# One chunk's residual on VectorE, an earlier load and sum of phi, and two pieces of TensorE work half a half slot later, in a one-core attention and mixer kernel

## The chip, the core and the metric

The kernel runs on one core of one Trainium2 chip. The core has a matrix engine (TensorE, PE in the profile, with PEld for its weight loads), three engines for elementwise work (VectorE or DVE, ScalarE or ACT, GpSimd or POOL), and SyncE (SP), which here only issues transfers. Each engine runs its own instructions in the order in which the program gives them, and waits at an instruction until what that needs is there. Transfers are issued by SP and by ACT and carried out by 16 DMA engines. The metric is the device time in microseconds of one execution, as the median of several.

## What is computed

The reference takes q, k, v and phi of 8 batches, 8 heads, 576 positions, and four weight matrices. Everything is in 32-bit floats.

```python
a = np.exp(phi - np.max(phi, axis=2, keepdims=True))        # over the 576 positions
a = a / (np.sum(a, axis=2, keepdims=True) + 1e-09)
k_m = np.einsum('bhsm,bhsd->bhmd', a, k)                    # 32 memory keys, 64 wide
v_m = np.einsum('bhsm,bhsd->bhmd', a, v)
scores = scale * np.matmul(q, k_m.transpose(0, 1, 3, 2))
attn = softmax(scores)                                      # over the 32 memories
x = np.matmul(attn, v_m)                                    # to (batch, 576, 512)
h = np.maximum(x.transpose(0, 2, 1) @ w_tok1, 0.0) @ w_tok2
u = x + h.transpose(0, 2, 1)
out = u + np.maximum(u @ w_ch1, 0.0) @ w_ch2                # 512 -> 1536 -> 512
```

## The kernel before

There are two streams of work. The first, by **quads**, is the attention and the token mixer: a quad is four heads of one batch, named (b, Q) with Q 0 or 1. The second, by **chunks**, is the channel mixer: the 8 x 576 positions are cut into nine chunks of 512, and each goes through the two big products with w_ch1 and w_ch2. The channel mixer is nearly all of TensorE's work, and the quads' small products are put in between.

Numbers are split into a high and a low part (`h`, `l`), each a float that the matrix engine's fast mode takes; a product is three matmuls, high by high, high by low, low by high. ScalarE makes the high part (a copy with rounding), VectorE or GpSimd the low part (a subtraction).

**The order.** Up to the end of chunk 0 a planner in the program orders the steps. After that the order is written out by hand. Time is counted in half slots h, 24 to a chunk. For chunks 1 and 2 a slot g covers h = 2g and 2g + 1: the first product of a hidden block (`ch1`, 12 matmuls into `cp`), then the second product of the block before it (`ch2`, 12 matmuls into `acc`). From h = 72 (chunk 3 on) `quarters` runs instead: it makes two hidden blocks at a time from seven smaller products (a recursive scheme on quarters of the matrices; tiles `qa`, `qb`, copied to `whole` by ScalarE), with the weights combined beforehand and loaded as `unit` tiles, issued by ScalarE, three ahead of their use.

Everything else is an event: `at(h, fn, *x, k=...)` enters a function under half slot h and a class k, and `run(h, ...)` calls what stands there. In a slot of chunk 1 or 2 `run` is called in this order: (2g - 1, 1), (2g - 0.5; -1, 0, 1), then the hidden block's high and low parts, (2g, 0), then `ch2`, then (2g, 1), (2g + 0.5; -1, 0, 1), (2g + 1; -1, 0). So an event at an even h with k = 0 is ahead of `ch2`, and with k = 1 behind it. Events of one h and k are called as they were entered, quad by quad.

**A quad's steps.** Each quad has a start m for its keys and values and a start r for its scores. The list `starts` (L1779 to L1782) gives, as (b, Q, m, r): (2, 0, 24, 24), (2, 1, 34, 34), (3, 0, 38, 44), (3, 1, 49, 54), (4, 0, 59, 63.5), (4, 1, 69, 74), (5, 0, 79, 86), (5, 1, 91, 98), and so on every 12 half slots to (7, 1, 139, 146). The steps, in the order in which data flows:

- `load_phi` (L405, a load of 320 KB on SP; two buffers, used in turn), `phi_max` (VectorE reduces over a partition's positions, then GpSimd does an all-reduce over partitions, `pr` and `prr`), `phi_sub` and `phi_only_exp`, `phi_sum` (the same with a sum, `pr` and `psr`).
- `step_kv` (L463): 40 small matmuls of phi by k and v into `kvp`. From quad (5, 0) on they stand inside `step_s` of the quad before (`follow`), at its r + 2. Then `spread_k`, at once for batch 2, later for the others (`scales`, `turn_keys`, `spread_v`, at m + 0.5 to m + 1.5). `turn_keys` stores the keys with four transfers on SP, `get_keys` at m + 3.5 loads them twice (`kb`). For batch 2 `step_T` at m + 1 turns them on TensorE (`Tp`). `load_kv` and `load_q` are on SP too.
- `step_s` at r + 2: scores into two banks `sp`; `turn_both` has VectorE turn them to `S` (L573), then `S_max`, `S_sub` (L583), `S_exp` on ScalarE, `S_sum`, `S_mul` (r + 2.5 to r + 4.5).
- `rows_out` at r + 4.5: four stores of S to DRAM on SP, and `rows_in` at r + 6, which loads them back as `raw` (L670, L673); `nat_full` and `nat_tail` (r + 8, r + 8.5) split `raw` into `nat`, on ScalarE and VectorE.
- `turn_pairs` at r + 5: `aT`; `a_pair` (L636) at r + 6 and r + 6.5: ScalarE copies the high part of one half of `aT` (L638), and GpSimd subtracts for the low part (L639). `v_pair` at r + 7 and r + 7.5: four ScalarE copies into `vv`, a tile that takes the room of `aT`, so they wait until `a_pair` has read it.
- `step_A` at r + 9.5 (needs `nat`), `step_R` at r + 10.5, and `step_u` in four parts from r + 12, 8 matmuls each into a bank `u`. ScalarE and VectorE take the result into the chunks' inputs `uh`, `ul` (or `u` and `rest`).

The small products share two PSUM banks (tag "at"), given out in turn: `kvp`, `Tp`, the two `sp`, `Ap`, `Rp` and each part of `u` take one, and wait until VectorE and ScalarE have read what was in it two takers ago.

**A chunk's end.** `residual` (L192) adds the two parts of the chunk's input again, four additions of 128 x 512, into a tile `o`; `add` (L200) adds the accumulated products when the chunk is done, and `store` writes it out. Chunks from 3 on keep their input whole and have no residual. For chunk 1 the residual stands at h = 44, for chunk 2 at h = 64 (`h - 8`), both on GpSimd.

The functions that the change touches, with the line numbers of the profile:

Of the kernel before, what the change touches and what calls it, by code (L numbers as in the profile page):

```python
# [28 lines left out]
def kernel(  # L29
# [25 lines left out]
    nc = tc.nc  # L55
# [10 lines left out]
    NF = 2 * w_ch2.shape[0]  # L66
# [3 lines left out]
    NKK = DM // P  # L70
# [5 lines left out]
    WIN, AHEAD = 3, 3  # L76
# [38 lines left out]
    def f32(t):  # L115
        return t.bitcast(F32)
# [16 lines left out]
    def wide(dtype, name):  # L133

        return sb.tile([P, NKK, CW], dtype, tag="wide", name=name, bufs=5)


    class Chunk:
# [50 lines left out]
                        stop=f == end - 1 and x == 2,  # L189
                    )  # L190

        def residual(s, channels=range(NKK)):  # L192
            for a in channels:
                if a == 0:
                    s.o = wide(F32, "o" + s.n)
                nc.gpsimd.tensor_tensor(
                    out=s.o[:, a], in0=f32(s.uh[:, a]), in1=f32(s.ul[:, a]), op=ALU.add
                )

# [127 lines left out]
    chunks = {}  # L327
# [1318 lines left out]
    a, c = quads[0, 0], quads[0, 1]  # L1646
# [80 lines left out]
    for Q, h0 in ((0, 3), (1, 11)):  # L1727
        qd = quads[1, Q]
# [46 lines left out]
    def at(h, fn, *x, k=0):  # L1775
        events.setdefault((max(h, 0), k), []).append((fn, x))
# [3 lines left out]
    while starts[-1][:2] != (B - 1, 1):  # L1780
        b, Q, m, r = starts[-1]
        starts.append((b + Q, 1 - Q, r + 5, r + NF))  # L1782
    for b, Q, m, r in starts:
        qd = second if b == 2 and not Q else Quad(b, Q)
        fine = b > 2
        if qd is not second:
            at(max(m - 11, 2 * NF), qd.load_phi)
            if fine:
                w = 1.5 * ((b, Q) == (5, 0))
                at(m - (6 if (b, Q) == (3, 0) else 8.5 - w), qd.phi_max, k=1)  # L1790
                w -= 1.5 * (JOINT < (b, Q))
                at(m - 4.5 + w, qd.phi_sub)
                at(m - 4 + w, qd.phi_only_exp)
                w += 1.5 * (JOINT < (b, Q))
                at(m - 3.5 + w, qd.phi_sum)
            else:
                at(m - 7, qd.phi_max, k=1)
                at(m - 3, qd.phi_exp, k=1)
                at(m - 2, qd.phi_sum, k=1)
            at(loaded + (5 if (b, Q) > (3, 1) else 1), qd.load_kv, k=1)  # L1800
            at(r - (3 if fine else 4), qd.load_q, k=1)
        joint = JOINT < (b, Q)
        if joint:
            former.follow, loaded = qd, m - 3
        else:
            at(m, qd.step_kv)
            loaded = m
        qd.follow, former = None, qd
        at(r + 2, qd.step_s)
        if fine:  # L1810
            for x, fn in (
                (m + 0.5, qd.scales), (m + 1, qd.turn_keys), (m + 1.5, qd.spread_v),
                (m + 3.5, qd.get_keys), (m + 5, qd.v_high), (m + 6, qd.v_low),
                (r + 2.5, qd.S_max), (r + 3, qd.sub_exp), (r + 4, qd.S_sum), (r + 4.5, qd.S_mul),
                (r + 4.5, qd.rows_out), (r + 5, qd.turn_pairs), (r + 8, qd.nat_full),
                (r + 8.5, qd.nat_tail), (r + 9.5, qd.step_A), (r + 10.5, qd.step_R),
            ):
                at(x, fn)
            at(r + 6, qd.rows_in, "qT", 1)
            for x in range(2):  # L1820
                at(r + 6 + x / 2, qd.a_pair, x)
                at(r + 7 + x / 2, qd.v_pair, x)
            for x in range(4):
                at(r + 12 + x // 2 * 1.5 + x % 2 / 2, qd.step_u, x // 2, x % 2)
            continue
        at(m + 4, qd.values)
        at(m + 1, qd.step_T)
        at(r + 3, qd.sm2)
        at(r + (3 if qd is second else 4), qd.a_pair, 1)
        at(r + 6, qd.nat, k=1)  # L1830
        at(r + 7, qd.v_pairs)
        at(r + 8, qd.step_A)
        at(r + 9, qd.step_R)
        for x in range(4):
            at(r + 10 + x // 2 * (1 if qd is second else 2), qd.step_u, x // 2, x % 2)
    for c in range(2, CHUNKS):
        h = 2 * NF * (c - 1)
# [18 lines left out]
    for c in range(CHUNKS - 1):  # L1856
        h = 2 * NF * (c + 1)
        if 0 < c < WIN:
            at(h - (8 if c == WIN - 1 else 4), lambda c=c: chunks[c].residual(), k=1)
        for x in range(NKK) if c < WIN - 1 else ():  # L1860
            at(h + 1, lambda c=c, x=x: chunks[c].add(x), k=-1)
        at(h + (3 if c < WIN - 1 else 4), lambda c=c: chunks[c].store(), k=1)
# [16 lines left out]
    for g in range(NF, NF * WIN):  # L1879
        c, f = g // NF, g % NF  # L1880
# [184 lines left out]
```

## Time and profile before

| what | us |
|---|---|
| median of 3 runs | 767.47 (766.58 to 768.25) |
| the profiled execution, whole | 765.93 |
| its span, first to last instruction | 764.1 |
| PE busy in it | 750.2 |
| DVE, ACT, POOL busy in it | 465.5, 338.2, 109.4 |
| mean granted PE clock | 0.997 |

The views that follow in the prediction are read like this. A row of the **timeline** gives the start in us from the span's start, the duration, the engine, the line, the operation, the tiles as out<-in with shapes, how many instructions were merged, and in brackets the engine's idle time before it with what ended that. A row of the **chain of waits** gives start, duration and what was running, for the work that ended last, followed back from the end. A row of the **waits** names who waited for whom, the total, the number of times and the longest. A row of the **groups** gives busy time and mean ns of one, and the idle time before them. A row of the **transfers** gives the queue that issued them, their number, the size of one and the median us from issue to landing. A q behind an engine's name is its sequencer, which issues transfers and waits. A releaser is inferred from the semaphores; where it had long been done, something else kept the engine. In time, h = 34 is near 165 us, h = 66 near 283 us, h = 72 near 303 us, and the phi maxima of the last four quads are at 387, 428, 469 and 511 us.

### The profile page before, as it was taken

What the parts mean: (1) busy time and instruction counts of PE and PEld (TensorE: products, weight loads), DVE (VectorE), ACT (ScalarE), POOL (GpSimd) and SP (SyncE); (2) the same over time, 40 slices, a digit from 0 to 9 for tenths busy, and PEclk for the clock granted to TensorE, in tenths of its full rate; (3) what the DMA queues carried; (4) which work ended last, traced back from release to release, by engine and by line L of the source; (5) the groups of instructions that cost most, each with busy time, mean ns of one, the idle gap of its engine ahead of it and who ended that gap; (6) DMA issues with size and microseconds to landing.
All of it is one profiled execution on the core that took longest, in us unless ns stands there. A gap on an engine that the chain in (4) does not pass through costs nothing.

```text
span 764.1 us, 13364 instructions
## 1 busy us (share of the span) xinstructions
PE 750.2 (98%) x5159; PEld 651.8 (85%) x5159; DVE 465.5 (61%) x876; ACT 338.2 (44%) x771; POOL 109.4 (14%) x94
## 2 busy tenths in 40 slices
PE   9999999999999999899999999999999999999998
PEld 8777788787877878789888889888989999998997
DVE  4989874787567655665676558554855255335234
ACT  5897553242414333454453536353635343333331
POOL 2144343011212123020101001010101000000000
PEclk9999999999999999999999999999999999999999
DMA  9954630673925445767576849584757367556651
GB/s 348 415 211 155 226 103 12 166 260 120 285 45 186 136 161 133 270 181 259 154 265 198 286 132 281 186 279 132 195 195 206 113 190 229 171 166 221 193 184 64
DMA packets 90447, 147.35 MB, mean 193 GB/s; under 512 B 41488, under 2 KB 60304, under 8 KB 86160
## 3 DMA queue, kind: packets, MB, share of 16 engines
q1 hardware_dynamic: 69216, 79.77, 31.4%
q10 hardware_dynamic: 21168, 66.73, 28.1%
q8 instruction: 41, 0.67, 0.4%
q14 instruction: 22, 0.18, 0.1%
HBM read 121.57 MB, written 24.90 MB: 192 GB/s over the span
## 4 chain that ended last, share of the span: by engine, by line
PE 78%; DVE 7%; DMA 5%; ACT 3%; issue 2%; SPq 2%; POOL 2%; ACTq 0%; DVEq 0%; POOLq 0%
PE acc L184 31%; PE qa L322 12%; PE qb L322 9%; PE cp L161 9%; PE u L748 8%; PE Ap L708 3%; DMA phi<-in_phi_dram 2%; PE u L1406 2%; PE Rp L727 1%; POOL a L639 1%; PE sp L566 1%; DMA rows<-S 1%; PE sp L467 1%; DMA raww<-in_w_tok_dram 1%; SPq L519 1%
## 5 line engine op out<-in xcount | busy, mean ns | idle before, releaser
L184 PE MATMUL acc<-qhh,c 128*128 128x512 f32 x376 | 145.6, 395 | 0.0
L322 PEld LDWEIGHTS qa<-xT,unit 128*128 128x128 f32 x648 | 91.8, 189 | 12.2 <-ACT whole L1915 2.9
L322 PEld LDWEIGHTS qb<-x,unit 128*128 128x128 f32 x648 | 91.7, 188 | 10.2 <-ACT whole L1915 0.8
L1918 DVE TENSOR_TENSOR whole<-whole 128x256 f32<-128x256 f32 x72 | 33.9, 471 | 107.5 <-ACT whole L1915 107.0
L322 PE MATMUL qa<-xT,unit 128*128 128x256 f32 x648 | 94.8, 282 | 2.2 <-ACT whole L1915 2.2
L184 PE MATMUL acc<-hh,c 128*128 128x512 f32 x288 | 96.5, 394 | 0.0
L322 PE MATMUL qb<-x,unit 128*128 128x256 f32 x648 | 94.4, 281 | 0.4 <-ACT whole L1915 0.4
L184 PEld LDWEIGHTS acc<-qhh,c 128*128 128x128 f32 x376 | 70.8, 188 | 11.8 <-issue 3.3
L1915 ACT COPY whole<-qa 128x256 f32<-128x256 f32 x108 | 40.1, 371 | 88.8 <-PE qa L322 88.7
L184 PE MATMUL acc<-qal,c 128*128 128x512 f32 x276 | 78.2, 394 | 0.0
L184 PE MATMUL acc<-qhl,c 128*128 128x512 f32 x188 | 75.0, 399 | 2.3 <-DVE qhl L129 2.3
L184 PEld LDWEIGHTS acc<-hh,c 128*128 128x128 f32 x288 | 54.1, 188 | 13.8 <-issue 2.9
L639 POOL TENSOR_TENSOR a<-aT,a 64x576 fp32r<-64x576 f32 x22 | 33.9, 1540 | 162.8 <-ACT a L638 135.9
L184 PE MATMUL acc<-hl,c 128*128 128x512 f32 x144 | 56.2, 390 | 0.0
L1915 ACT COPY whole<-qb 128x256 f32<-128x256 f32 x72 | 26.6, 370 | 62.8 <-PE qb L322 62.8
L161 PE MATMUL cp<-uh,c1h 128*128 128x512 f32 x144 | 51.4, 397 | 0.0
L161 PE MATMUL cp<-ul,c1h 128*128 128x512 f32 x144 | 50.3, 390 | 0.0
L161 PE MATMUL cp<-uh,c1l 128*128 128x512 f32 x144 | 50.3, 390 | 0.0
L184 PEld LDWEIGHTS acc<-qal,c 128*128 128x128 f32 x276 | 46.2, 189 | 4.2
L129 DVE SCALAR_TENSOR_TENSOR hl<-cp,hh 128x512 fp32r<-128x512 f32 x36 | 24.7, 687 | 37.7 <-ACT hh L126 37.6
L129 DVE SCALAR_TENSOR_TENSOR qhl<-whole,qhh 128x256 fp32r<-128x256 f32 x72 | 32.2, 447 | 21.4 <-ACT qhh L126 21.3
L126 ACT ACTIVATE qhh<-whole 128x256 fp32r<-128x256 f32 x72 | 30.2, 420 | 23.3 <-DVE whole L1918 15.9
(239 smaller groups left out, 1448.2 us busy)
## 6 DMA issues: line engine op xcount, KB each, us to landing
unit<-sums ACTq DMA_DIRECT2D x108, 512.0 KB, 3.9
kv<-in_kv_dram SPq DMA_DIRECT2D x12, 1280.0 KB, 7.7
rawc<-in_w_ch_dram SPq DMA_DIRECT2D x12, 1024.0 KB, 10.6
q<-in_q_dram SPq DMA_DIRECT2D x16, 576.0 KB, 6.9
unit<-sums ACTq DMA_DIRECT2D x36, 256.0 KB, 3.5
sums<-sums SPq DMA_DIRECT2D x12, 512.0 KB, 6.1
phi<-in_phi_dram SPq DMA_DIRECT2D x16, 320.0 KB, 3.8
out_dram<-u SPq DMA_DIRECT2D x5, 1024.0 KB, 4.2
```

What stands on the lines that cost most here:

```text
L126: nc.scalar.activation(out=h, in_=ps, func=AF.Relu)
L129: nc.vector.scalar_tensor_tensor(out=l, in0=ps, scalar=0.0, in1=f32(h), op0=ALU.max, op1=ALU.subtract)
L161: nc.tensor.matmul(ps, l[:, a, w], r[:, a], start=n == 0, stop=n == len(mm) - 1)
L184: nc.tensor.matmul(ps, l_[f // 2][:, f % 2, a * P : (a + 1) * P], r[:, w], start=f == start and x == 0, stop=f == end - 1 and x == 2,)
L322: nc.tensor.matmul(ps[:, :HW], l, r, start=first and n == 0, stop=n == len(mm) - 1, skip_group_check=not first,)
L467: nc.tensor.matmul(s.kvp[32 * i : 32 * i + 32, : 2 * D], s.pt[:, i, j, :], s.kv[:, :, j, i, :], start=j == 0, stop=j == NC - 1,)
L639: s.low_eng.tensor_tensor(out=l, in0=s.aT[own], in1=f32(h), op=ALU.subtract)
L708: nc.tensor.matmul(ps[:, :TT], a, w, start=x == 0, stop=x == len(mm) - 1)
L748: nc.tensor.matmul(ps[:, :HALF], a, r, start=x == 0, stop=x == len(mm) - 1)
L1406: nc.tensor.matmul(ps[:, :HALF], a, r, start=n == 0, stop=n == len(mm) - 1)
L1915: nc.scalar.copy(out=to, in_=ps[:, :HW])
L1918: nc.vector.tensor_tensor(out=to, in0=x, in1=y, op=ALU.add)
```

## The change

```diff
-        def residual(s, channels=range(NKK)):
+        def residual(s, channels=range(NKK), eng=nc.gpsimd):
             for a in channels:
                 if a == 0:
                     s.o = wide(F32, "o" + s.n)
-                nc.gpsimd.tensor_tensor(
+                eng.tensor_tensor(
                     out=s.o[:, a], in0=f32(s.uh[:, a]), in1=f32(s.ul[:, a]), op=ALU.add
                 )
...
-            at(max(m - 11, 2 * NF), qd.load_phi)
+            at(max(m - (16 if b > 4 else 11), 2 * NF), qd.load_phi)
...
                 w += 1.5 * (JOINT < (b, Q))
-                at(m - 3.5 + w, qd.phi_sum)
+                at(m - 3.5, qd.phi_sum)
...
-            at(m, qd.step_kv)
+            at(m + (b == 2) * Q / 2, qd.step_kv)
...
-                at(r + 12 + x // 2 * 1.5 + x % 2 / 2, qd.step_u, x // 2, x % 2)
+                at(r + 12 + x // 2 * 1.5 + x % 2 / 2, qd.step_u, x // 2, x % 2, k=int((b, Q, x) == (3, 1, 0)))
...
         if 0 < c < WIN:
-            at(h - (8 if c == WIN - 1 else 4), lambda c=c: chunks[c].residual(), k=1)
+            for x in ([0, 1], [2, 3]) if c == WIN - 1 else ():
+                at(h - 5.5 + x[0] / 4, lambda c=c, x=x: chunks[c].residual(x, nc.vector), k=1)
+            if c < WIN - 1:
+                at(h - 4, lambda c=c: chunks[c].residual(), k=1)
```

It has five parts:

- **Residual of chunk 2.** Its four additions go from GpSimd to VectorE, and from h = 64 to h = 66.5 (two) and 67 (two), behind all other events of those half slots. Chunk 1's stays as it was.
- **Load of phi.** For the quads of batches 5, 6 and 7 (six loads) it is issued at m - 16 and no longer at m - 11. In the program's order that is before `rows_out` of the quad two before and before the stores of the keys of the quad one before, which used to be ahead of it.
- **Sum of phi.** The `phi_sum` of quad (5, 0) goes from m - 2 to m - 3.5, that is from h = 77 to 75.5. For all other quads the old formula gave m - 3.5 already.
- **Keys' products of the third batch's second quad.** `step_kv` of (2, 1), with its `spread_k`, goes from h = 34, ahead of the second product of slot 17, to h = 34.5, behind it.
- **First part of u of quad (3, 1).** It stays at h = 66, and goes from k = 0 to k = 1, that is from ahead of the second product of slot 33 to behind it; its copies move with it.

No instruction is added or taken away, apart from the engine that does the residual.

## The prediction

> **What bounds the kernel now.** I read the page's busy times first, then whom TensorE waited for, then the chain of waits around the longest of those waits, then the timelines of the engines named in it.
>
> ```profile
> PE 750.2 (98%) x5159; PEld 651.8 (85%) x5159; DVE 465.5 (61%) x876; ACT 338.2 (44%) x771; POOL 109.4 (14%) x94
> ```
>
> TensorE (PE) is busy for 98% of the span, and the change takes no matmul away. It can win only what PE loses by waiting. The view of PE's waits (total us, times, longest):
>
> ```profile
> PE acc L184 <- DVE qhl L129: 2.3, 3, 1.4
> PE qa L322 <- ACT whole L1915: 2.2, 1, 2.2
> ...
> PE kvp L467 <- DVE ul L216: 1.0, 1, 1.0
> PE u L748 <- DVE S L573: 0.7, 1, 0.7
> ...
> PE qb L322 <- ACT whole L1915: 0.4, 1, 0.4
> ```
>
> These five rows are 6.6 us, and every edit lies beside one of them. The 2.2 us end a chain that GpSimd (POOL) begins: first the chain's rows, then POOL's timeline, then two stretches (busy us of PE, PEld, DVE, ACT and POOL, PE's granted clock, DMA share, GB/s):
>
> ```profile
> 301.15 0.67 ACT a L638
> ...
> 304.56 1.43 POOL a L639
> ...
> 306.01 0.30 ACT vv L652
> ...
> 307.25 0.34 ACT nat L122
> ...
> 307.78 0.37 ACT whole L1915
> ...
> 308.20 1.28 PE qa L322 x6
> ```
>
> ```profile
> 283.31 5.54 POOL L196 TENSOR_TENSOR o<-uh,ul 128x512 f32<-128x512 f32 x4 [7.42 <-DMA kv<-in_kv_dram]
> 294.82 1.09 POOL L454 PARTITION_ALL_REDUCE psr<-pr  x1 [5.97 <-DVE hl L129]
> 302.86 3.12 POOL L639 TENSOR_TENSOR a<-aT,a 64x576 fp32r<-64x576 f32 x2 [6.95 <-ACT xT L271]
> ...
> 328.31 1.08 POOL L454 PARTITION_ALL_REDUCE psr<-pr  x1 [15.34 <-issue]
> 336.93 3.07 POOL L639 TENSOR_TENSOR a<-aT,a 64x576 fp32r<-64x576 f32 x2 [7.54 <-ACT whole L1915]
> ```
>
> ```profile
> 308.20:312.20 4.00, 4.00 (x21) 4.00 (x22) 3.85 (x7) 2.13 (x6) 0.00 (x0) 0.57 0.78 225
> 307.90:320.10 12.20, 11.90 (x81) 11.47 (x82) 11.00 (x21) 6.80 (x19) 0.72 (x1) 0.86 0.91 322
> ```
>
> Between an all-reduce and a tensor operation, in either order, POOL always stands idle for 6 to 7.5 us here (5.97, 6.95, 7.42, 7.54). The releasers named beside these four differ and had long been done, so I read the idle time as POOL's own cost of switching. The residual (L196) stands between two all-reduces, so it costs POOL 5.54 us of work and two switches, and pushes the low parts `a` (L639) to 302.86. ScalarE (ACT) may overwrite `aT` with `vv` only when POOL is through with it at 305.98; `nat` and the copy `whole` queue behind, and PE waits until 308.20. Behind that wait PE's granted clock is 0.57 on the mean of 4.0 us.
>
> **The change part by part.** Every sum is against this execution: span 764.1 us, 765.93 us with what lies around it. The median of the three runs, 767.47, is 1.54 above; I take the savings from it unchanged.
>
> **A, the keys' products of quad (2,1), h 34 to 34.5.** They now stand behind the second product of slot 17. PE's row, then rows of the chain of waits, then DVE's timeline:
>
> ```profile
> 166.45 1.30 PE L467 MATMUL kvp<-kv,phi 128*32 128x128 f32 x40 [0.99 <-DVE ul L216]
> ```
> ```profile
> 170.67 2.11 PE u L748 x16
> ...
> 276.11 2.75 PE acc L184 x12
> ```
> ```profile
> 168.08 0.41 DVE L496 TENSOR_TENSOR vb<-kvp,ms 128x256 f32<-128x256 f32 x1
> ...
> 169.88 1.35 DVE L421 TENSOR_REDUCE pr<-phi 128x128 f32<-128x640 f32 x1
> 172.19 0.46 DVE L216 TENSOR_TENSOR ul<-u,uh 128x288 fp32r<-128x288 f32 x1 [0.96 <-ACT uh L213]
> ```
>
> The wait of 0.99 goes: 12 matmuls of `acc` (2.75) need nothing late and start near 165.4, the products near 168.15, two parts of u near 169.5, and PE is free for the turn `Tp` at 171.6. The turn takes the bank of the first of these parts, and that is free only after DVE's `ul`. DVE must before that scale keys and values (done about 0.7 after the products, 170.3) and reduce phi (1.3, to 171.6), which used to end a microsecond before `ul`; `ul` ends near 172.05, and the turn starts at 172.1. Today it starts after 166.45 + 1.3 + 2.75 + 2.1 = 172.6 or a little later. Gain 0.6 (bounds 0 and 1.0).
>
> **B, first part of u of quad (3,1), behind the second product of slot 33.**
>
> ```profile
> 283.63 0.37 PE L748 MATMUL u<-a,vv 128*128 128x288 f32 x1 [0.67 <-DVE S L573]
> ```
>
> u waits for DVE to turn the scores out of its bank. Behind the 12 matmuls of `acc` (2.75) the bank is long free, and those need only slot 32's hidden pieces. u's copies move with it and reach ACT ahead of the exponential of S, as before. Gain 0.65 (0 to 0.7).
>
> **C, the residual of chunk 2.** Four 128x512 additions come to DVE at h 66.5 and 67.
>
> ```profile
> 286.38 1.32 DVE L583 TENSOR_TENSOR S<-S,mx 128x576 f32<-128x576 f32 x1
> 289.85 0.75 DVE L592 TENSOR_REDUCE sm<-S 128x18 f32<-128x576 f32 x1 [2.15 <-ACT S L588]
> ```
> ```profile
> L348 DVE TENSOR_TENSOR w<-c1h,c1l 128x512 f32<-128x512 f32 x12 | 8.8, 776 | 0.0
> ```
>
> The same shape from SBUF is 0.776 us in row L348, so at most 3.1 us. They stand just between these two DVE rows, where DVE idles 2.15 us; what is over, about 1 us, makes the row sum later, and behind it the next low part and S's scaling, unless the subtraction gets shorter without the residual running on POOL (1.32 us beside it; nothing here bounds that from above). Nothing there is on PE's path. If the cover were gone, `rows_out` would start up to 3.1 us later.
>
> On POOL the all-reduce needs only DVE's reduction, which stands ahead of the subtraction, so it is done before 286.4. So the switch ends by about 286.4 + 1.1 + 7 = 294.5, 8 us before today's 302.86, and the low parts wait for ACT alone. The second one starts when ACT's copy ends (301.15 + 0.67 = 301.82) and ends 1.43 later, near 303.3 and not 305.98: 2.6 us off a chain on which PE waits 2.2. What is late next is `raw`:
>
> ```profile
> 294.87 2.47 SPq L663 DMA_DIRECT2D rows<-S  x4
> 302.32 0.38 SPq L670 DMA_DIRECT2D raw<-rows  x1
> ```
> ```profile
> raw<-rows SPq DMA_DIRECT2D x1, 256.0 KB, 3.6
> ```
>
> It lands at 302.32 + 3.6 = 305.9, and `nat` on ACT, ahead of `whole`, needs it. If nothing of that moved, PE would still go on only 0.05 + 0.34 + 0.18 + 0.37 + 0.05 = 1.0 later, at 306.9, so 1.3 of the 2.2 us would be won. But phi of quad (5,0) no longer follows `rows` onto the DMA engines at h 68 (it goes at h 63), and POOL's switch no longer falls beside them, so I expect `raw` before 304.3, in time. Then the idle 2.2 goes, and the half clock behind it: (1 - 0.57) x 4.0 = 1.7. Of these 3.9 I take 0.4 back, since in the next stretch DVE is busy for 11.00 of 12.20 us, and phi's subtraction for the joint products behind that stretch comes through its queue; PE would come to it sooner than DVE. Gain 3.5; bounds 1.3 (the transfer stays and so does the half clock) and 3.9.
>
> [...]
>
> **D, phi's sum of quad (5,0), h 77 to 75.5.** Its all-reduce at 328.31 makes POOL late for the next `a` at 336.93, and PE waits 0.4 at `qb` behind the same chain.
>
> ```profile
> 322.07 0.85 DVE L573 STREAM_TRANSPOSE S<-sp 128x288 f32<-128x288 f32 x2 [2.43 <-PE sp L566]
> ```
>
> At its new place the 1.35 us reduction falls into this 2.43 us idle of DVE. The switch is then over before ACT's copy, and 0.4 us of idle and about 0.25 of restarting go. Gain 0.65 (0 if ACT's copy is the later one; and below nothing, about -0.5, if DVE stands at the reduction for the exponential of phi, in front of work that PE needs).
>
> **E, phi loaded 5 half slots sooner for batches 5 to 7.**
>
> ```profile
> 388.07 0.39 PE L184 MATMUL acc<-qhh,c 128*128 128x512 f32 x1
> 388.96 0.50 PE L184 MATMUL acc<-qhl,c 128*128 128x512 f32 x1 [0.50 <-DVE qhl L129]
> ```
> ```profile
> 387.24 1.34 DVE L421 TENSOR_REDUCE pr<-phi 128x128 f32<-128x640 f32 x1 [1.61 <-DMA phi<-in_phi_dram]
> ```
> ```profile
> DVE pr L421 <- DMA phi<-in_phi_dram: 6.6, 5, 2.2
> ```
>
> The load is issued on SP behind four stores of keys that themselves wait for DVE, and DVE stands at the maximum of phi (6.6 us in five places, longest 2.2) with the low part `qhl` behind it, for which PE waits in three of them. At m - 16 `rows_out` and the stores of keys come behind the load on SP, and phi's buffer (two in turn) was released by products ten half slots before, so the load waits for nothing and holds up nothing there. Its 320 KB leave the burst of keys, kv and q and go to a stretch with unit loads. DVE's wait covers PE's in each: at 388 DVE would be done 1.6 earlier, PE needs 0.5. A matmul follows another after 2.75 / 12 = 0.23; 388.07 to 388.96 is 0.89, so the stall is 0.66, and restarting adds the 0.11 by which the matmul is longer: 0.27 more than the idle shown. Three of them: 2.3 + 3 x 0.27 = 3.1. Gain 3.1 (bounds 0 and 3.1).
>
> **Sum:** 0.6 + 0.65 + 3.5 + 0.65 + 3.1 = 8.5. The profiled execution comes to 757.4, the median to 767.47 - 8.5 = **759.0 us**.
>
> **The rivals.**
>
> *The transfer takes POOL's place* (chance 0.22). `raw` lands near 305.9, PE still waits 1.0 at `qa`. For it: four stores of rows need 7.4 us from their first issue to 302.3, in a stretch full of transfers. Against it: that stretch loses a load and a switch. Time: 759.0 + 0.9, or 761.6 with the whole half clock kept; I put 760.8.
>
> *The half clock stays though the gap goes* (0.05). If the throttle comes from more than this gap, 1.7 of C is not won: 760.7. [...]
>
> *Phi waits are replaced* (0.10). Where DVE stops waiting for phi, ACT's `qhh` or a unit comes last, and E gives nothing: 762.1. For it: DVE's release and ACT's are close in those stretches. Against it: DVE's wait is the one that PE's row names.
>
> *The stalls are this one execution's* (0.04). The median is 1.54 above it; were the waits accidents, the change would not do what it says, and the time stays near 767.
>
> *Slower: ACT stops at its DMA issues* (0.05).
>
> ```profile
> ACT qhh L126 <- DMA unit<-sums: 4.1, 2, 2.4
> ```
> ```profile
> unit<-sums ACTq DMA_DIRECT2D x108, 512.0 KB, 3.9
> kv<-in_kv_dram SPq DMA_DIRECT2D x12, 1280.0 KB, 7.7
> ```
>
> ACT issues unit loads itself, and already stood up to 2.4 us for an earlier transfer before going on. Moving phi's issue changes which transfer an issue must wait for; behind kv's 7.7 in place of a unit's 3.9 ACT stands 3.8 longer, in front of the copies PE needs, and a gap of that size brings the half clock: 3.8 + 1.7 = 5.5 in each of the five stretches whose phi moves. E's 3.1 would be gone, the other 5.4 stay. From the first such stretch on nothing is left, with two it is 767.47 - 5.4 + 11 = 773.1. Against it: the two waits of today are short and let PE through.
>
> **How the numbers follow.** My forecast has 0.54: 759.0, its own range 757.5 to 760.5. With the rivals at 760.8 (0.22), 760.7 (0.05), 762.1 (0.10), 767 (0.04) and 773.1 (0.05), a range of 757.0 to 762.6 takes in the first four cases and leaves out the last two and some of the edges; its lower end is A at its bound of 1.0, C and E in full and half a microsecond of scatter (the three runs span 1.7). About 0.2% (1.5 us) is what a measurement can tell from no change: faster by more 0.90, within 0.05, slower 0.05.
>
> **What would show it.** Right: POOL's row L454 stands directly behind DVE's reduction near 286 and L639 near 298; no PE wait over 1 us at `qa`, no clock below 1 between 303 and 760; `kvp <- DVE ul` and `u <- DVE S` gone from PE's waits; no `pr <- DMA phi` on DVE. Wrong: `nat <- DMA raw` on ACT before `qa`; a wait of `Tp` over 0.6; ACT waiting for DMA around 380 to 510; or a PE gap over 2 us anywhere new.

## The result, and the profile after

| what | before | after |
|---|---|---|
| median, us | 767.55 (766.58 to 768.25, 4 runs) | 759.83 (758.15 to 760.23, 4 runs) |
| ratio of the times | | 0.9896 (95% interval 0.9878 to 0.9915) |
| the profiled execution, whole | 765.93 | 759.66 |
| its span | 764.1 | 757.9 |
| mean granted PE clock | 0.997 | 1.0 |

The change is 7.7 us faster by the medians and 6.3 by the two profiled executions; 8.5 was forecast for both. One execution of the kernel before, at 776.33 us, ran in a slower state and is left out of the ratios and ranges below. The waits of PE after (us in total, times, longest), to be read against the five rows of before (the first, at the start, is the same 1.6 in both):

```profile
PE pp L1085 <- POOL mask L91: 1.6, 1, 1.6
PE Ap L708 <- ACT nat L122: 1.3, 1, 1.3
PE Ap L708 <- DVE nat L123: 0.7, 3, 0.2
```

All five are gone from the list: `qhl`, `qa`, `kvp`, `u` and `qb`. One of 1.3 is new: `Ap` waits for `nat`, the split of `raw`. Two more views, POOL's timeline after, and then the stretch in which PE's granted clock was 0.57 (it stands behind the five engines' busy times):

```profile
284.85 1.08 POOL L454 PARTITION_ALL_REDUCE psr<-pr  x1 [9.40 <-DVE pr L421]
297.39 1.42 POOL L639 TENSOR_TENSOR a<-aT,a 64x576 fp32r<-64x576 f32 x1 [11.46 <-DVE ps L479]
300.89 1.43 POOL L639 TENSOR_TENSOR a<-aT,a 64x576 fp32r<-64x576 f32 x1 [2.08 <-ACT a L638]
...
317.18 1.08 POOL L454 PARTITION_ALL_REDUCE psr<-pr  x1 [8.27 <-issue]
331.92 3.00 POOL L639 TENSOR_TENSOR a<-aT,a 64x576 fp32r<-64x576 f32 x2 [13.67 <-ACT a L638]
```

```profile
308.20:312.20 4.00, 4.00 (x32) 3.83 (x31) 4.00 (x8) 2.25 (x6) 0.71 (x1) 1.00 1.01 373
```

The all-reduce stands at 284.85, ten microseconds ahead of its old place, and the low parts `a` are done at 302.3 in place of 306.0. The clock stays at 1.00. The second sum of phi (317.18) and the low parts behind it (331.92) are early too.

To put a size on each step I compared where the same matmul (the n-th of the 5159) starts in the two traces. These are positions, at times of after, and not a view of the profile:

| stretch | after minus before, us | change in it |
|---|---|---|
| up to 163 (start-up) | +0.58 | +0.58; the trace's record of the granted clock begins at 6.46 in place of 4.86 |
| `Tp` at 172.4, step A | -0.30 | -0.88 |
| `u` at 287, step B | -1.01 | -0.71 |
| behind `Ap` at 308, step C | -4.54 | -3.53 |
| joint products at 316 | -4.14 | +0.40 |
| behind `qb` at 338, step D | -4.95 | -0.81 |
| behind `Ap` at 344, the new wait | -2.92 | +2.03 |
| behind the four waits for phi, 385 to 508 (three in the list of before, one of 0.2 below it), step E | -6.28 | -3.36 |
| last matmul | -6.28 | 0 |

So each of the five parts gave about what was worked out for it, and one new stall of 2.0 took a quarter of it back. Where it comes from stands in the chain of waits of after:

```profile
330.81 4.78 DMA rows<-S
...
335.71 4.75 DMA raw<-rows
...
340.48 0.63 ACT nat L122
...
341.13 0.70 DVE nat L123
...
341.87 1.22 PE Ap L708 x8
```

The load `raw` of quad (4,1) took 4.75 us, where the median of such loads is 3.6. One row of ACT's timeline names a load that was under way beside it:

```profile
335.90 0.33 ACTq L392 DMA_DIRECT2D unit<-sums  x1
```

A unit load of 512 KB was issued 0.19 us behind `raw`, and took 4.4 us.

### The profile page after: what moved, and what is told of

The parts are those of the page before. It is cut to its first block, busy times and chain, and to the rows that moved or that the text cites. A ratio compares the mean times of both kernels' runs of the same rounds, so it can differ in the third digit from the quotient of the medians.

```text
span 757.9 us, 13366 instructions
## 1 busy us (share of the span) xinstructions
PE 748.8 (99%) x5159; PEld 651.2 (86%) x5159; DVE 468.6 (62%) x880; ACT 338.3 (45%) x771; POOL 103.6 (14%) x90
## 4 chain that ended last, share of the span: by engine, by line
PE 79%; DVE 8%; DMA 6%; issue 2%; ACT 2%; SPq 1%; POOL 1%; ACTq 0%; POOLq 0%; DVEq 0%
PE acc L184 32%; PE qa L322 12%; PE qb L322 9%; PE cp L161 8%; PE u L748 8%; PE Ap L708 3%; DMA raw<-rows 2%; DMA rows<-S 2%; PE u L1406 2%; DMA k<-in_kv_dram 1%; PE Rp L727 1%; PE sp L566 1%; PE sp L467 1%; DMA sums<-c1h 1%; PE end L184 1%
```

## The experiments

Each kernel was run beside the kernel before on the same chip, whose median there lay between 767.52 and 768.83; ratios are to that. Where a gain is given in us, it is the ratio's share of 767.5, unless two medians are named.

### One part at a time

The residual's move alone, on the kernel before (the last part of the diff above and the engine argument; one line of it):

```diff
...
+                at(h - 5.5 + x[0] / 4, lambda c=c, x=x: chunks[c].residual(x, nc.vector), k=1)
...
```

> The kernel before with the residual's move alone (VectorE, h 66.5 and 67). Theory (GpSimd's switch between all-reduce and tensor operation held up the low parts): GpSimd's all-reduce of the sum stands right behind VectorE's reduction near 286, its first low part near 298, and TensorE's wait of 2.2 us at qa and the half clock behind it go or shrink: 2.3 to 3.4 us faster, less what quad (4, 1) gives back when TensorE comes sooner to its nat: 764.3 to 766. Phi of quad (5, 0) still follows the rows here, so raw may land at 305 and keep up to 1 us of the wait. Rival (the wait is set by rows and raw, not by GpSimd): the wait at qa stays over 1.5 us, 767 or more.

766.09 us, ratio 0.9960 (0.9943 to 0.9978), some 3.1 us won, as the theory had it. PE's waits in its profile:

```profile
PE acc L184 <- DVE qhl L129: 5.3, 4, 2.2
...
PE kvp L467 <- DVE ul L216: 1.0, 1, 1.0
PE qa L322 <- ACT whole L1918: 0.9, 1, 0.9
```

The gap at `qa` falls from 2.2 to 0.9, since `raw` is now the last to arrive (`nat` on ScalarE waits 1.35 for it), and the clock is not halved (its mean is 1.0 in this execution). The waits for phi grow from 2.3 to 5.3 in this execution, which at 767.39 is a long one of its kernel.

The phi loads alone:

```diff
-            at(max(m - 11, 2 * NF), qd.load_phi)
+            at(max(m - (16 if b > 4 else 11), 2 * NF), qd.load_phi)
```

> The kernel before with the six loads of phi at m - 16 alone. Theory (VectorE stood for phi in front of qhl): no wait of VectorE for phi, no wait of TensorE for qhl, 3.1 us faster: 764.4. Rival (ScalarE's qhh or a unit comes last in its place): waits of TensorE for qhl stay, at most 1 us faster: 766.5 to 767.5.

763.65 us, ratio 0.9926 (0.9903 to 0.9948): 5.7 us by the ratio, well above the 3.1 of the theory, whose waits were the right ones. No wait for `qhl` is left. The gap at `qa` is still there, and it is longer than before:

```profile
PE qa L322 <- ACT whole L1915: 2.5, 1, 2.5
```

Yet behind it the clock is not halved (the same columns as above):

```profile
306.70:309.30 2.60, 0.30 (x2) 0.00 (x0) 0.07 (x1) 1.91 (x6) 0.60 (x1) 1.00 0.27 78
309.30:312.70 3.40, 3.18 (x23) 3.05 (x24) 3.34 (x6) 2.06 (x7) 0.00 (x0) 1.00 0.81 215
```

TensorE's two moves alone:

```diff
-            at(m, qd.step_kv)
+            at(m + (b == 2) * Q / 2, qd.step_kv)
...
+                at(r + 12 + x // 2 * 1.5 + x % 2 / 2, qd.step_u, x // 2, x % 2, k=int((b, Q, x) == (3, 1, 0)))
```

> The kernel before with the two moves on TensorE alone (keys' products of (2, 1) and the first part of u of (3, 1)). Both waits (0.99 and 0.67 us) are gone from TensorE's list. Theory: the first gives 0.85 us to the end; the second is given back at qa near 305, since GpSimd's chain there starts before it: TensorE's wait at qa grows from 2.2 to about 2.8; together 0.8 to 0.9 us faster, 766.6. Rival (both are kept): 1.5 us faster, 766.0.

767.10 us, ratio 0.9976 (0.9956 to 0.9995), 1.8 us. The waits of `kvp` and `u` are gone, and `qa` keeps its 2.2 and its half clock:

```profile
308.00:312.00 4.00, 4.00 (x20) 3.71 (x19) 4.00 (x7) 1.61 (x5) 0.72 (x1) 0.58 0.91 277
```

What I had put down as B being given back at `qa` didn't happen; PE kept both gains up to the waits for phi. There they were lost in this execution, whose waits for `qhl` come to 3.4.

### The residual's place or its engine

The changed kernel with the residual at its new place, but on GpSimd:

```diff
-                at(h - 5.5 + x[0] / 4, lambda c=c, x=x: chunks[c].residual(x, nc.vector), k=1)
+                at(h - 5.5 + x[0] / 4, lambda c=c, x=x: chunks[c].residual(x, nc.gpsimd), k=1)
```

> The kernel after with one word changed: the residual goes back to GpSimd but stays at its new place (h 66.5 and 67), behind the all-reduce of the sum and ahead of the low parts. So GpSimd does the same 5.5 us of work as before, but without a switch of its own. Theory (the two switches, not the work, were the price): GpSimd does the residual near 293 to 298.5 after one switch, the second low part stays near 301 to 302.5, and the time is that of the kernel after within 0.5 us: 759.3 to 760.3. Rival (GpSimd's work or its contention with VectorE held the low parts up): the wait at qa comes back with over 1.5 us, 761.5 to 763.5.

764.32 us, ratio 0.9936 (0.9913 to 0.9960), between before and after, and slower than the theory (up to 760.3) and the rival (up to 763.5) both had it. POOL's timeline:

```profile
285.18 1.08 POOL L454 PARTITION_ALL_REDUCE psr<-pr  x1 [9.40 <-DVE pr L421]
293.57 6.83 POOL L196 TENSOR_TENSOR o<-uh,ul 128x512 f32<-128x512 f32 x4 [7.32 <-issue]
300.48 3.33 POOL L639 TENSOR_TENSOR a<-aT,a 64x576 fp32r<-64x576 f32 x2
```

With the additions beside the other tensor operations there are two switches fewer than before (none ahead of this all-reduce, none between the additions and the low parts), the low parts end at 303.8, and the gap at `qa` is 0.2. So it was the two switches that had made them late, as the prediction read it; GpSimd's work is the same. But PE now waits elsewhere (1.5 at `acc` for `hl`, 2.5 at the joint products for the load `kv`), and VectorE's timeline shows why; first this kernel, then after:

```profile
295.91 1.65 DVE L267 TENSOR_TENSOR t<-t,u 128x512 f32<-128x512 f32 x1
297.48 1.78 DVE L276 TENSOR_TENSOR x<-u,x 128x512 fp32r<-128x512 f32 x1
```

```profile
286.71 2.49 DVE L196 TENSOR_TENSOR o<-uh,ul 128x512 f32<-128x512 f32 x4
...
295.32 0.69 DVE L267 TENSOR_TENSOR t<-t,u 128x512 f32<-128x512 f32 x1
295.93 0.69 DVE L276 TENSOR_TENSOR x<-u,x 128x512 fp32r<-128x512 f32 x1
```

Beside GpSimd's additions the same VectorE operations take 1.65 and 1.78 in place of 0.69, and the additions 6.83 in place of the 5.54 of before. The low part `hl` comes at 304.3, the keys' stores at 305.5 and the load `kv` behind them at 311.1. On GpSimd the residual costs switches or VectorE's time, according to its place; on VectorE it costs 2.49 us in a stretch where that engine was idle.

The changed kernel with the residual at its old place, h = 64 on GpSimd:

```diff
+            at(h - (8 if c == WIN - 1 else 4), lambda c=c: chunks[c].residual(), k=1)
```

(in place of the four lines of the change), beside the changed kernel itself:

> The changed kernel itself, on the same chip as the next three, so that they have a fellow to be measured against. Both theories: 0.990 of the kernel before, within 0.2%; a wait of Ap for nat near 341 us of 1.3, because nat on ScalarE waits for raw.

> The changed kernel with the residual of chunk 2 back on GpSimd at h = 64. Theory (with phi's loads moved, nothing behind the end of chunk 2 swallows what the residual's move wins): 2.2 to 3.9 us slower than the changed kernel, 2.2 if the gap at qa is spared the half clock by its place in the clock's window, 3.9 if not. Rival (the wait for raw one quad later, 1.8 us, fills up whatever is won before it, so part of the move is worth nothing): 0.4 to 2.0 us slower, and no wait of Ap for nat near 341.

The changed kernel: 758.72 us, 0.9879 (0.9848 to 0.9909), with a wait of `Ap` of 1.5. With the residual back: 762.17, 0.9921 (0.9897 to 0.9945). So the move is worth 3.45 us inside the whole, the theory's 2.2 to 3.9 and not the rival's 2.0 at most, although the wait of `Ap` near 341 is gone, as the rival had it (one of 0.9 stands near 425, at quad (5,1)). In its profile the gap is back (`qa`, 2.8), and the half clock with it:

```profile
308.00:312.00 4.00, 4.00 (x21) 4.00 (x22) 3.74 (x7) 2.12 (x6) 0.00 (x0) 0.60 0.81 231
```

### What the earlier loads win

The kernel before, with the loads where they were, and only the maximum of phi later by one half slot, for the last five quads:

```diff
-                at(m - (6 if (b, Q) == (3, 0) else 8.5 - w), qd.phi_max, k=1)
+                at(m - (6 if (b, Q) == (3, 0) else 7.5 if b > 4 and w == 0 else 8.5 - w), qd.phi_max, k=1)
```

> The kernel before with one edit: the maximum of phi of the last five quads one half slot later, at m - 7.5, and the loads left where they were. phi is subtracted 4.4 us after the all-reduce ends (394.0 against 389.5), so 1.7 us of that can be spent. Theory (what the earlier loads win is that VectorE no longer stands at phi in front of low parts that PE needs): 2.5 to 5 us faster than before, no wait of acc for qhl over 0.5. Rival (the loads win by lying elsewhere among the transfers): within 1 us of before, waits for qhl gone but others in their place.

762.93 us, ratio 0.9934 (0.9909 to 0.9959): 5.1 us, as much as the loads, and no wait for `qhl`. VectorE's timeline shows the order that does it:

```profile
386.87 0.43 DVE L129 SCALAR_TENSOR_TENSOR qhl<-whole,qhh 128x256 fp32r<-128x256 f32 x1 [1.20 <-ACT qhh L126]
...
388.48 1.32 DVE L421 TENSOR_REDUCE pr<-phi 128x128 f32<-128x640 f32 x1
```

The low part now stands ahead of the reduction. So the price was VectorE standing at phi in front of work that PE needs; with the loads left among the transfers where they were, 5.1 of the loads' 5.7 is won.

Why 5 and not 3.1? I took a second profile of the kernel before:

> The kernel before once more, for a second profile of it. Theory (its waits for phi are set by how the transfers fall in each execution, and the one profiled at first, 765.93 us, was a lucky one): in an execution of 768 us or more PE's waits for qhl come to 3.5 us or more in place of 2.3. Rival (they are fixed, and the longer executions are long from elsewhere, as the half clock): 2.1 to 2.6.

```profile
PE acc L184 <- DVE qhl L129: 3.6, 4, 1.6
PE qa L322 <- ACT whole L1915: 2.2, 1, 2.2
...
PE qb L322 <- ACT whole L1915: 1.1, 1, 1.1
```

At 768.77 us, nearer the medians, the waits for phi are 3.6, in four places, and the wait at `qb` is 1.1; `qa`, `kvp` and `u` are the same. Of these two profiles the first, at 765.93, shows both waits that vary at the smaller size. The kernel before ranged from 764.3 to 773.9, the changed one from 757.3 to 760.3.

The changed kernel without the earlier loads:

```diff
-            at(max(m - (16 if b > 4 else 11), 2 * NF), qd.load_phi)
+            at(max(m - 11, 2 * NF), qd.load_phi)
```

> The changed kernel with phi's six loads back at m - 11, so that the other four parts stand alone. Theory (what the four parts win is given back at the waits for phi, which the transfers time): 1 to 2.5 us faster than the kernel before, and 4 us or more of waits for qhl. Rival (the parts add up: the residual alone won 0.4% and TensorE's two moves 0.24%, that is 4.9 us): 4 to 6 us faster than the kernel before, waits for qhl of 2.3.

762.82 us, ratio 0.9942 (0.9925 to 0.9959): 4.5 us faster than before, which is the rival's 4 to 6. Its profiled execution, at 764.84 a long one, has 4.1 us of waits for `qhl`, the theory's mark. So the waits for phi do take something back from PE in single executions, but by the medians the four other parts keep what they win. The four, without the loads, win 4.5; the residual alone and TensorE's two moves alone won 3.1 + 1.8 = 4.9.

### The new wait

Three edits of the changed kernel change what happens around `raw`. Half a half slot later for `nat` and the two products of quad (4,1):

```diff
+            l = 0.5 * ((b, Q) == (4, 1))
...
-                (r + 4.5, qd.rows_out), (r + 5, qd.turn_pairs), (r + 8, qd.nat_full),
-                (r + 8.5, qd.nat_tail), (r + 9.5, qd.step_A), (r + 10.5, qd.step_R),
+                (r + 4.5, qd.rows_out), (r + 5, qd.turn_pairs), (r + 8 + l, qd.nat_full),
+                (r + 8.5 + l, qd.nat_tail), (r + 9.5 + l, qd.step_A), (r + 10.5 + l, qd.step_R),
```

> The changed kernel with quad (4,1)'s split of raw and its two products Ap and Rp half a half slot later, so that other work stands before them while raw is on its way. Theory (ScalarE's wait for raw, 2.5 us, is what holds PE near 340): 1.2 to 1.8 us faster than the changed kernel, wait of Ap gone. Rival (the wait only moves to Rp, to the first part of u, or to the copies that queue behind nat): within 0.5 us of the changed kernel, with a new PE wait of about 1 between 340 and 350.

The phi load of (5,0) alone back (`16 if (b, Q) > (5, 0) else 11`):

> The changed kernel with the phi load of quad (5,0) alone back at m - 11, where it follows the four stores of rows onto the DMA engines. Theory (that load beside raw is what would make raw the last at qa): raw lands near 305, ScalarE's nat waits 1 to 2 us, PE waits 0.5 to 1.0 at qa, and the kernel is 0.5 to 1.0 us slower. Rival (raw is late from the stores before it, not from phi): raw lands near 304.2 as in the changed kernel, no wait at qa, within 0.3 us.

The phi sum of (5,0) back:

```diff
-                at(m - 3.5, qd.phi_sum)
+                at(m - 3.5 + w, qd.phi_sum)
```

> The changed kernel with the sum of phi of quad (5,0) back at h = 77. The time can't tell 0.65 us, so the profile is read. Theory (its all-reduce keeps GpSimd from the next low parts): the all-reduce stands near 325 and the low parts near 333 to 334 in place of 331.9, PE waits 0.2 to 0.5 at qb and stands 0.4 to 0.7 later there; the unit load, which goes by PE, then falls further behind raw, so that the wait of Ap for nat near 341 shrinks below 1.3. Rival (GpSimd is early enough either way): low parts at 332, no wait at qb, wait of Ap 1.3 to 1.5 as before.

The first came to 758.88 us (0.9878, 0.9848 to 0.9908), the second to 758.67 (0.9879, 0.9848 to 0.9910), both the same as the changed kernel's 758.72; the third to 759.89 (0.9868, 0.9833 to 0.9903), beside a before of 768.83. None is told apart from the changed kernel by its time, so the 1.2 to 1.8 us that the first was to win did not come. Their profiles say more.

In the second, PE waits 0.8 at `qa` and `raw` is there at 305.2, the theory's mark. But in the third, whose phi load is the early one, `raw` is there at 305.2 too and PE waits 1.1, so that phi makes `raw` late isn't shown; nor is a loss seen in the time. In the third, POOL's timeline is as the theory had it:

```profile
325.21 1.08 POOL L454 PARTITION_ALL_REDUCE psr<-pr  x1 [16.02 <-DVE pr L421]
333.74 3.01 POOL L639 TENSOR_TENSOR a<-aT,a 64x576 fp32r<-64x576 f32 x2 [7.45 <-ACT whole L1918]
```

and PE waits 0.23 at `qb` and stands 0.43 later there, 0.67 with the slower matmuls behind it (six of `qb` take 0.98 in place of 0.87). In all three the wait at `Ap` near 341 is gone, in the first for a reason that was not the edit's: its `raw` had landed at 338.8, a microsecond before ScalarE came to it. One reading is that the wait goes by how close a unit load is issued to `raw`. The times of issue and landing in the traces, for the profiled executions:

| kernel, quad | `raw` issued | unit load issued, behind `raw` by | `raw` took, us | PE at `Ap` |
|---|---|---|---|---|
| before, (4,1) | 338.52 | 2.46 | 2.9 | no wait |
| after, (4,1) | 335.71 | 0.19 | 4.7 | 1.3 |
| after again, (4,1) | 337.15 | -0.61 | 4.2 | 1.5 |
| residual back, (4,1) | 338.88 | 0.81 | 2.9 | no wait |
| `nat` later, (4,1) | 335.88 | 1.05 | 2.9 | no wait |
| first load back, (4,1) | 335.46 | 1.63 | 3.2 | no wait |
| sum back, (4,1) | 335.58 | 2.15 | 3.2 | no wait |
| all loads back, (4,1) | 335.28 | 1.38 | 2.9 | no wait |
| maximum later, (5,1) | 421.96 | 0.08 | 4.5 | 1.1 |
| residual alone, (4,1) | 338.77 | 0.34 | 3.0 | no wait |
| loads alone, (5,1) | 421.85 | 0.34 | 3.2 | no wait |
| residual back, (5,1) | 420.04 | 0.24 | 4.5 | 0.9 |
| sum back, (5,1) | 417.25 | 0.98 | 4.8 | 0.5 |
| all loads back, (5,1) | 418.23 | 1.10 | 4.8 | 0.4 |

The first nine rows look like a rule: with the unit load 0.8 us or more behind it `raw` takes 2.9 to 3.2 us, with the two within 0.6 of each other 4.2 to 4.7, and PE waits. The last five break it: at 0.34 `raw` took 3.0 and 3.2, at about 1.0 it took 4.8. So the distance to that unit load doesn't decide by itself, no run holds that load back alone, and what makes `raw` late stays open. What the traces show is that `raw` takes from 2.8 to 5.2 us at (4,1), (5,1) and (6,1), and that where PE waited at `Ap` for 0.4 or more it had taken over 4.

## Why the prediction was right, and where it was not

**A and B** (0.6 and 0.65): 0.88 and 0.71 by position. The chain of after runs as it was worked out: `ul` from 171.99 to 172.36 and the turn at 172.41, where 172.05 and 172.1 were forecast for an execution that started 0.58 sooner. Alone the two are worth 1.8 us by the median (0.4 to 3.4).

**C** (3.5): 3.53 up to 308, less 0.40 given back at the joint products, as the prediction took off; that is 3.13 net; 3.1 alone, 3.45 within the whole by the medians. The mechanism is shown from both sides: two switches taken away by place (on GpSimd) or by engine, and `qa`'s gap shrinks to 0.2 or 0. VectorE paid 2.49 us where 3.1 at most was allowed, and the subtraction beside it fell from 1.32 to 0.76, the slowing beside GpSimd's work of which the prediction had one sign.

**Half clock.** The forecast that it follows the gap held in this kernel, but the gap's length doesn't decide it: behind 2.2 us the clock was halved before (0.57), and behind 2.5 with the loads alone it was not (1.00). In 15 executions of the kernel before, taken beside the changed kernel, the mean granted clock was 1.0 in seven. So 1.7 of C's 3.5 depended on something that the prediction didn't have: in the traces it went with where the gap lay on a grid of 3.41 us, as the last section shows. That the profiled execution had the half clock was chance.

**D** (0.65): 0.81 by position; undone, 0.67 up to the same matmul.

**E** (3.1): 3.36 by position, but by the medians 5.7 alone and 4.1 within the whole (762.82 less 758.72). This term was mis-sized, and its bound with it. The step that failed is to take the waits for phi of one execution as those of the median: "I take the savings from it unchanged". They vary, 2.3 and 3.6 in two profiles, and that execution was 1.5 below its median. The mechanism was right, as the maximum's move shows, and so was the price of one stall: 0.27 more than the idle shown was worked out, and at 388 PE won 0.77 where 0.50 was shown.

**What wasn't in the sum**: the wait for `raw` one quad later, 2.0. The rival that `raw` would take POOL's place named the right transfer at quad (4,0), where it lost: `nat` waited 0.62 for it on ScalarE, and PE lost 0.3. In other executions of nearly the same kernel PE waited there 0.3 (the changed kernel again) to 1.1 (sum back), so that rival was near; one of the prediction's own signs of being wrong, `nat` waiting for `raw` ahead of `qa`, did show. The prediction asked what would be late next at (4,0) and didn't ask it at (4,1), although that PE would come to `nat` there over 4 us sooner was in its sum.

**Too high and too low.** The median came out 0.8 from the forecast, while the profiled execution (757.4 forecast, 759.66) missed by 2.3. By the medians E won 1.0 to 2.6 more than its term, and the new wait cost 2.0 in the profiled execution; if it stands in the median as well, the two nearly cancel. That it does isn't shown, since three kernels whose profiles have no such wait near 341 have about the same medians. Either way the fit of the median is in part luck.

**The slower rival** did not come. ScalarE stands somewhat longer at unit loads before `qhh` (4.1 us in two places before, 5.9 in three after, 2.4 and 2.5 at the longest), and PE doesn't wait for it.

## What to carry to other kernels

An in-order engine that may stand at a transfer should have ahead of it, in its own queue, all that the bound engine needs soon: here moving the waiting instruction back by half a slot won 5.1 us, and loading earlier 5.7. Ask of every stretch behind a gain, not only of the next one, what now comes last: here the wait for the same kind of load came up at a later quad. And size a wait that ends on a transfer from several executions, since one profile shows one draw (2.3 and 3.6 us for phi in two of the kernel before).

## What the hardware showed that was not expected

- **In these traces the half clock lay on a fixed grid of 3.41 us.** Gaps at `qa` of 2.2 and 2.8 us gave 0.58 and 0.60 over 308 to 312 (TensorE's moves alone, residual back), a gap of 2.5 gave 1.00 over 309.3 to 312.7 (loads alone). In the traces' records of the granted clock each half-clocked stretch at `qa` is 3.41 us long and begins a whole number of 3.4133 us behind the first record: 308.65 - 4.86 = 303.79 = 89 x 3.4133 in the kernel before, 307.76 - 7.39 = 300.37 = 88 x 3.4133 with the residual back. The half clock at the end of the execution lies on the same grid: 762.62 - 4.86 = 757.76 = 222 x 3.4133 before, and 757.39 - 6.46 = 750.93 = 220 x 3.4133 after. Cut along that grid (the columns as above), the gap of before lies in one window, and that of the loads alone, whose first record is at 7.76, is shared by two, with the border at 7.76 + 88 x 3.4133 = 308.13. The kernel before comes first, then the loads alone:

```profile
305.24:308.65 3.41, 1.25 (x7) 0.77 (x7) 0.71 (x2) 2.58 (x9) 0.74 (x1) 1.00 0.39 104
308.65:312.06 3.41, 3.41 (x19) 3.41 (x18) 3.38 (x6) 1.68 (x4) 0.00 (x0) 0.50 0.82 238
```

```profile
304.72:308.13 3.41, 2.28 (x14) 1.68 (x12) 0.00 (x0) 0.77 (x3) 2.51 (x2) 1.00 0.33 86
308.13:311.54 3.41, 2.02 (x17) 2.02 (x18) 2.25 (x4) 3.07 (x9) 0.00 (x0) 1.00 0.70 202
```

  PE is idle for 2.16 of 3.41 us in the window of before, with the half clock right behind it, and for 1.13 and 1.39 in the two of the loads alone, whose clock stays at 1.00 from 303 to 757. More windows on the grid, from before and then from after:

```profile
510.04:513.46 3.42, 2.04 (x12) 1.56 (x11) 2.20 (x4) 0.93 (x3) 0.73 (x1) 1.00 0.96 384
513.46:516.87 3.41, 3.41 (x25) 3.19 (x24) 1.76 (x4) 1.33 (x4) 0.00 (x0) 1.00 0.95 325
759.21:762.62 3.41, 1.51 (x13) 1.31 (x11) 1.54 (x3) 0.00 (x0) 0.00 (x0) 1.00 0.64 231
762.62:764.13 1.51, 0.00 (x0) 0.00 (x0) 0.00 (x0) 0.00 (x0) 0.00 (x0) 0.50 0.00 0
```

```profile
753.98:757.39 3.41, 0.46 (x4) 0.26 (x3) 0.64 (x2) 0.00 (x0) 0.00 (x0) 1.00 0.44 154
757.39:757.87 0.48, 0.00 (x0) 0.00 (x0) 0.00 (x0) 0.00 (x0) 0.00 (x0) 0.50 0.00 0
```

  So windows with 1.90, 2.16 and 2.95 us of idle were followed by the half clock, and those with 1.13, 1.38 and 1.39 were not. Between 1.39 and 1.90 these views show nothing.
- **GpSimd stood idle at every switch,** 7.32 us from the all-reduce to the additions at the residual's new place and 7.45 from the all-reduce to the low parts with the sum back, like the four of before. The shortest idle time at any change between an all-reduce and a tensor operation is 5.82 in the profile of before and 5.81 in that of after. Two all-reduces follow each other after 0.20 (before, at 162.49), and the low parts follow the additions at the new place after 0.08.
- **VectorE slowed by a factor of 2.4 to 2.6** beside GpSimd's additions (0.69 to 1.65 and 1.78), and GpSimd's four additions take 6.83 there, against 5.54 at their old place, where VectorE's subtraction beside them took 1.32.
